# Moving the x buffers by 64 bytes in SBUF with two unused tiles

## The chip, the cores and the metric

The kernel runs on one core of a Trainium2 chip. The metric is device time in microseconds (us), the median over timed runs; less is better. One more execution is taken with the hardware profiler, and its trace is what is read below. The engines are named as in the profile: PE (TensorE, matmuls), PEld (TensorE's weight loads, which run beside its matmuls), DVE (VectorE), ACT (ScalarE), POOL (GpSimd), SP (SyncE, which issues most DMAs).

## What is computed

A gated linear attention over 768 positions (2 batches, 8 heads of 40), and behind it two feed-forward layers on 1536 tokens of width 320 with an inner width of 2048. All arrays are fp32.

```python
def reference(**kwargs):
    attn_out = _attn_ref(q, k, v, i_gate, f_gate, o_gate)        # a scan over t with gates
    x = attn_out.transpose(0, 2, 1, 3).reshape(1536, 320)
    h = x @ w_in                                                 # layer 1: 320 -> 2048
    g = np.where(h >= 1, h, np.where(h <= -1, 0.0, (h + 1) ** 2 / 4))
    x = g @ w_out                                                # 2048 -> 320
    h = x @ w2_in                                                # layer 2
    g = np.maximum(h, 0.0) + np.log1p(np.exp(-np.abs(h)))
    return g @ w2_out
```

## The kernel before, in words

**Split operands.** Each matmul of the feed-forward layers works on fp32 numbers that are split in a high and a low part, and sums three products: high by high, high by low, low by high. x has its high part in the tiles xh0 to xh2 and its low part in xl0 to xl2, one pair for each block of 512 tokens. A weight tile w holds the high parts of one of 16 slices of the inner width (384 columns for the way up, 320 for the way down) and behind them the low parts. The activations g are split into gh and gl (`split_g`, L811).

**The loops.** `steps` (L929) runs over the 2 layers, in each over the 3 blocks, in each over the 16 slices. A step has these parts:

- `up` (L756): 8 matmuls into one PSUM tile h, all recorded under L767. Each streams 512 columns of xh or xl against a 128 by 128 piece of w, which a weight load has put in place. TensorE loads the piece for the next matmul while the present one streams.
- the activation on ACT and DVE (`hinge` or `softplus`), and `split_g`.
- three steps later (`LAG`) the way down. In layer 1 `down1` (L826) has 8 matmuls (L836 to L842) that stream 512 columns of gh or gl against pieces of w, and sum in the PSUM tile D. In layer 2 `down2` (L880) has 12 (L897 to L899) that stream 320 columns of w against pieces of gh or gl, into A and D.

So the three kinds of matmuls differ in what streams: x in `up`, gh and gl in `down1`, w in `down2`.

**Handing over a block.** After the last `down1` of a block, `to_x` (L845) writes its sum back into xh and xl by ACT (L853, L861) and DVE (L857, L865), and only then may the next block's `down1` write D.

**The order.** All instructions stand in an order that the class `Plan` works out in advance with costs of its own (`plan.run`, L976); it knows nothing of addresses. Each engine then takes its list in that order and waits on semaphores.

**Where tiles lie.** A pool gets its place in SBUF when it is opened, and the tiles of a pool lie one behind another in the order of the code, so the x tiles lie in the pool `const` behind the tiles of L232 to L241, and raw, v, w, u, gh, gl in pools behind `const`. A row of xh or xl that one matmul streams is 512 x 4 = 2048 bytes in a partition, a piece of w or gh that one load fetches 128 x 4 = 512 bytes, and the parts of w begin at multiples of 256 bytes in it. An operand therefore begins at the same place modulo 256 as its tile.

The lines of `up` that name its operands, and the declaration of the x tiles:

```python
            ops = [(w[:, a + 128 * k:a + 128 * k + 128], xs) for k in range(2)
                   for a, xs in ((0, xh[j][:, k]), (0, xl[j][:, k]), (lo, xh[j][:, k]))]
            ops += [(w[:, a + 256:a + 384], xh[j][:, 2]) for a in (0, lo)]
            for i, (a, x) in enumerate(ops):
                nc.tensor.matmul(hp, a, x, start=(i == 0), stop=(i == len(ops) - 1))
...
    state = const.tile([128, H, V1], F32)
    xh = [const.tile([128, 3, n], F32R, name=f"xh{j}") for j, (_, n) in enumerate(BLOCKS)]
    xl = [const.tile([128, 2, n], F32R, name=f"xl{j}") for j, (_, n) in enumerate(BLOCKS)]
```

Of the kernel before, what the change touches and what calls it, by code (L numbers as in the profile page):

```python
# [7 lines left out]
F32 = mybir.dt.float32  # L8
# [201 lines left out]
def mlstm_moe_moe(ctx: ExitStack, tc: tile.TileContext, gates, late, qk, tok, ident, w1, w2, out):  # L210
    nc = tc.nc

    def pool(name, bufs, stack=ctx, **kw):
        return stack.enter_context(tc.tile_pool(name=name, bufs=bufs, **kw))
# [5 lines left out]
    const = pool("const", 1)  # L220
# [17 lines left out]
    gr = const.tile([128, EARLY * C], F32)  # L238
    is_col = const.tile([128, NC, H], F32)
    state = const.tile([128, H, V1], F32)  # L240
    xh = [const.tile([128, 3, n], F32R, name=f"xh{j}") for j, (_, n) in enumerate(BLOCKS)]  # L241
    xl = [const.tile([128, 2, n], F32R, name=f"xl{j}") for j, (_, n) in enumerate(BLOCKS)]
    scr_d = [dram.tile([n, 16, C], F32, name=f"scr_d{s}") for s, n in enumerate((4, 8))]
    scr_f = dram.tile([NC - EARLY, 16, C], F32)

# [816 lines left out]
```

## Time and profile before

| | us |
|---|---|
| median of 3 runs | 432.34 |
| lowest, highest | 432.06, 433.53 |
| span of the profiled execution | 429.5 |
| PE busy in it | 409.7 |
| DVE busy | 295.2 |
| ACT busy | 260.1 |

The median lies 2.8 us above the profiled span. The page of the profile gives busy times, and the chain of work that ended last: from the last instruction back, at each step to what released it. A busy matmul row is longer than what a matmul costs in a stream of them, because matmuls overlap in the pipeline; the cost of one is the distance from its start to the next one's start, and that is what is read below from the chain and from the timeline.

The execution has four stages: to about 60 us attention with the first matmuls of layer 1; from there to 113 us attention, layer 1 and the weights' DMAs together; from 113 to 263 us layer 1; from 263 to 424 us layer 2; then 5.5 us for the last output.

### The profile page before, as it was taken

What the parts mean: (1) busy time and instruction counts of PE and PEld (TensorE: products, weight loads), DVE (VectorE), ACT (ScalarE), POOL (GpSimd) and SP (SyncE); (2) the same over time, 40 slices, a digit from 0 to 9 for tenths busy, and PEclk for the clock granted to TensorE, in tenths of its full rate; (3) what the DMA queues carried; (4) which work ended last, traced back from release to release, by engine and by line L of the source; (5) the groups of instructions that cost most, each with busy time, mean ns of one, the idle gap of its engine ahead of it and who ended that gap; (6) DMA issues with size and microseconds to landing.
All of it is one profiled execution on the core that took longest, in us unless ns stands there. A gap on an engine that the chain in (4) does not pass through costs nothing.

```text
span 429.5 us, 8096 instructions
## 1 busy us (share of the span) xinstructions
PE 409.7 (95%) x3299; PEld 340.3 (79%) x3299; DVE 295.2 (69%) x479; ACT 260.1 (61%) x447; POOL 37.2 (9%) x46
## 2 busy tenths in 40 slices
PE   7988779999899999999999999999999999999994
PEld 5555558877788888887888888999989999899994
DVE  4687998999868556556878787655565555655552
ACT  3255867768666446889889755555555555555551
POOL 3333122213101000000000000000000000000001
PEclk9999969999999999999999999999999999999999
DMA  8979595797912001644344000000020000110002
GB/s 289 343 260 318 156 295 177 213 321 221 304 66 74 2 2 51 193 162 136 134 134 137 0 2 0 1 2 0 2 61 2 0 2 0 36 27 2 0 2 61
DMA packets 13685, 44.93 MB, mean 105 GB/s; under 512 B 2320, under 2 KB 3984, under 8 KB 13648
## 3 DMA queue, kind: packets, MB, share of 16 engines
q1 hardware_dynamic: 12832, 43.22, 31.2%
q10 hardware_dynamic: 752, 1.03, 0.9%
q8 instruction: 26, 0.43, 0.4%
q0 software_dynamic: 64, 0.16, 0.2%
q14 instruction: 11, 0.09, 0.1%
HBM read 42.36 MB, written 2.05 MB: 103 GB/s over the span
## 4 chain that ended last, share of the span: by engine, by line
PE 77%; DMA 8%; DVE 6%; ACT 4%; issue 1%; SPq 1%; POOL 0%; DVEq 0%; POOLq 0%
PE h L767 36%; DMA raw<-in_w_dram 5%; PE D L841 4%; PE D L840 4%; PE D L842 4%; PE D L897 3%; PE D L899 3%; PE D L898 3%; PE A L898 3%; PE A L899 3%; PE A L897 3%; PE D L836 2%; PE D L837 2%; DMA f<-scr_f 2%; ACT v L715 1%
## 5 line engine op out<-in xcount | busy, mean ns | idle before, releaser
L767 PE MATMUL h<-xh,w 128*128 128x512 f32 x576 | 182.6, 400 | 1.5 <-DVE w L747 1.1
L767 PEld LDWEIGHTS h<-xh,w 128*128 128x128 f32 x576 | 108.7, 189 | 26.8 <-DVE w L747 3.0
L820 DVE TENSOR_TENSOR gl<-u,gh 128x512 fp32r<-128x512 f32 x96 | 67.5, 704 | 39.6 <-ACT gh L816 38.4
L816 ACT CAST gh<-u 128x512 fp32r<-128x512 f32 x96 | 59.4, 619 | 46.7 <-DVE u L807 34.0
L767 PE MATMUL h<-xl,w 128*128 128x512 f32 x192 | 76.3, 397 | 1.4 <-DVE xl L698 1.4
L807 DVE TENSOR_TENSOR u<-u,e 128x512 f32<-128x512 f32 x48 | 33.3, 693 | 29.2 <-ACT e L803 29.2
L803 ACT ACTIVATE e<-e 128x512 f32<-128x512 f32 x48 | 30.3, 632 | 37.6 <-DVE e L798 37.6
L775 ACT ACTIVATE u<-h 128x512 f32<-128x512 f32 x48 | 28.5, 595 | 25.9 <-PE h L767 25.6
L767 PEld LDWEIGHTS h<-xl,w 128*128 128x128 f32 x192 | 36.4, 190 | 8.0 <-DVE xl L698 1.8
L784 DVE SCALAR_TENSOR_TENSOR u<-u,h 128x512 f32<-128x512 f32 x48 | 32.7, 682 | 13.9 <-ACT u L780 13.7
L841 PE MATMUL D<-gh,w 128*128 128x512 f32 x96 | 37.9, 395 | 0.0
L840 PE MATMUL D<-gh,w 128*128 128x512 f32 x96 | 37.8, 394 | 0.0
L842 PE MATMUL D<-gl,w 128*128 128x512 f32 x96 | 37.5, 391 | 0.0
L798 DVE SCALAR_TENSOR_TENSOR e<-u,h 128x512 f32<-128x512 f32 x48 | 33.0, 687 | 6.0 <-ACT u L794 1.0
L726 DVE SCALAR_TENSOR_TENSOR v<-raw,v 128x704 int32<-128x704 int32 x32 | 28.6, 895 | 9.8 <-ACT v L719 8.8
L794 ACT ACTIVATE u<-h 128x512 f32<-128x512 f32 x48 | 28.7, 598 | 10.6 <-PE h L767 10.3
L747 DVE TENSOR_TENSOR w<-v,w 128x64 fp32r<-128x64 f32 (+2 forms) x45 | 30.2, 701 | 2.4 <-ACT w L738 2.4
L715 ACT ACTIVATE v<-raw 128x704 f32<-128x704 int8 x32 | 27.1, 849 | 7.3 <-DMA raw<-in_w_dram 5.4
L780 ACT ACTIVATE u<-u 128x512 f32<-128x512 f32 x48 | 30.2, 630 | 0.4
L897 PE MATMUL D<-w,gh 128*128 128x320 f32 x96 | 29.6, 309 | 0.1
L899 PE MATMUL D<-w,gl 128*128 128x320 f32 x96 | 29.7, 309 | 0.0
L898 PE MATMUL A<-w,gh 128*128 128x320 f32 x96 | 29.7, 309 | 0.0
(120 smaller groups left out, 611.5 us busy)
## 6 DMA issues: line engine op xcount, KB each, us to landing
raw<-in_w_dram SPq DMA_DIRECT2D x32, 704.0 KB, 4.8
qx<-in_qk_dram SPq DMA_DIRECT2D x12, 640.0 KB, 7.2
tok<-in_tok_dram SPq DMA_DIRECT2D x12, 496.0 KB, 6.0
dec<-scr_d SPq DMA_DIRECT2D x16, 128.0 KB, 6.7
f<-scr_f SPq DMA_DIRECT2D x16, 128.0 KB, 6.7
out_dram<-o SPq DMA_DIRECT2D x20, 80.0 KB, 2.1
dec<-scr_d ACTq DMA_DIRECT2D x6, 128.0 KB, 7.0
consts<-in_ident_dram SPq DMA_DIRECT2D x1, 164.0 KB, 4.0
```

The source lines that it names most:

```text
L767: nc.tensor.matmul(hp, a, x, start=(i == 0), stop=(i == len(ops) - 1))
L784: nc.vector.scalar_tensor_tensor(out=tiles[U], in0=tiles[U], scalar=1.0, in1=tiles[HP], op0=ALU.min, op1=ALU.max)
L798: nc.vector.scalar_tensor_tensor(out=new("e", E, [128, n]), in0=tiles[M], scalar=-2.0, in1=tiles[HP], op0=ALU.mult, op1=ALU.add)
L807: nc.vector.tensor_tensor(out=tiles[M], in0=tiles[M], in1=tiles[E], op=ALU.add)
L816: nc.scalar.copy(new("gh", GH, [128, n], F32R), tiles[G])
L820: nc.vector.tensor_tensor(out=new("gl", GL, [128, n], F32R), in0=tiles[G], in1=tiles[GH].bitcast(F32), op=ALU.subtract)
L840: nc.tensor.matmul(d[i], hi[:, k], gh, start=s, stop=False)
L841: nc.tensor.matmul(d[i], lo[:, k], gh, start=False, stop=False)
L842: nc.tensor.matmul(d[i], hi[:, k], gl, start=False, stop=e)
L897: nc.tensor.matmul(d, gh[:, k], hi, start=s, stop=False)
L898: nc.tensor.matmul(d, gh[:, k], lo, start=False, stop=False)
L899: nc.tensor.matmul(d, gl[:, k], hi, start=False, stop=e)
```

## The change

```diff
     state = const.tile([128, H, V1], F32)
+    const.tile([128, 16], F32, name="gap0")
     xh = [const.tile([128, 3, n], F32R, name=f"xh{j}") for j, (_, n) in enumerate(BLOCKS)]
     xl = [const.tile([128, 2, n], F32R, name=f"xl{j}") for j, (_, n) in enumerate(BLOCKS)]
+    const.tile([128, 48], F32, name="gap1")
```

Two tiles are declared in `const` that nothing reads or writes: 64 bytes in a partition ahead of the x tiles, 192 bytes behind them. In the built programs the tiles begin at these bytes of a partition:

| tile | before | modulo 256 | after | modulo 256 |
|---|---|---|---|---|
| xh0 | 23360 | 64 | 23424 | 128 |
| xl0 | 41792 | 64 | 41856 | 128 |
| raw, first | 54080 | 64 | 54336 | 64 |
| w, slice 0 of layer 1 | 121728 | 128 | 121984 | 128 |
| gh, first | 167296 | 128 | 167552 | 128 |
| gl, first | 175488 | 128 | 175744 | 128 |

All xh and xl tiles share the place of xh0 modulo 256, and all tiles of w, gh and gl that of the first. So the x tiles move by 64 bytes; all that lies behind them moves by 256 and keeps its place modulo 256; all ahead of them stays. No instruction is added, taken away or moved: the lists of all five engines, with their waits, are the same in both programs but for line numbers (up by one or two) and the numbers in names.

## Rows read from the trace of the kernel before

**Rows 1.** The page: busy time by engine, and shares of the chain that ended last.
```profile
PE 409.7 (95%) x3299; PEld 340.3 (79%) x3299; DVE 295.2 (69%) x479; ACT 260.1 (61%) x447; POOL 37.2 (9%) x46
...
PE 77%; DMA 8%; DVE 6%; ACT 4%; issue 1%; SPq 1%; POOL 0%; DVEq 0%; POOLq 0%
```

**Rows 2.** Windows, three stages: length, busy (instructions) by engine, PEclk, DMA share, GB/s.
```profile
183.30:200.22 16.92, 16.64 (x72) 13.16 (x72) 10.15 (x15) 14.38 (x25) 0.00 (x0) 1.00 0.54 174
200.22:262.88 62.66, 62.52 (x278) 51.08 (x278) 50.02 (x73) 48.76 (x80) 1.71 (x1) 1.00 0.20 70
262.88:424.04 161.16, 161.12 (x899) 145.72 (x899) 94.39 (x139) 82.89 (x137) 0.58 (x1) 1.00 0.04 9
```

**Rows 3.** Windows of line 767 alone (`up`): busy and count of matmuls, of loads.
```profile
60.00:113.06 53.06, 20.98 (x78) 14.04 (x76) 0.97 0.78 241
113.06:183.30 70.24, 36.03 (x142) 26.43 (x142) 1.00 0.27 86
183.30:200.22 16.92, 9.98 (x40) 7.49 (x40) 1.00 0.54 174
200.22:262.88 62.66, 32.29 (x128) 23.98 (x128) 1.00 0.20 70
262.88:424.04 161.16, 86.81 (x344) 62.98 (x344) 1.00 0.04 9
```

**Rows 4.** Windows of line 836 alone (once in each `down1`).
```profile
113.06:183.30 70.24, 6.91 (x17) 3.20 (x17) 1.00 0.27 86
...
200.22:262.88 62.66, 6.31 (x16) 2.97 (x16) 1.00 0.20 70
```

**Rows 5.** The chain in time, layer 1: start us, length us, what.
```profile
204.14 1.86 PE h L767 x8
...
252.24 1.86 PE h L767 x8
...
255.94 3.73 PE h L767 x16
```

**Rows 6.** The chain in time, layer 2.
```profile
263.58 1.86 PE h L767 x8
...
328.55 1.85 PE h L767 x8
...
415.12 1.86 PE h L767 x8
```

**Rows 7.** Timeline of PE, a `down1` behind another: start us, modelled length, what.
```profile
85.03 0.39 PE L840 MATMUL D<-gh,w 128*128 128x512 f32 x1
85.27 0.39 PE L841 MATMUL D<-gh,w 128*128 128x512 f32 x1
...
85.72 0.39 PE L836 MATMUL D<-gh,w 128*128 128x512 f32 x1
...
87.53 0.39 PE L767 MATMUL h<-xh,w 128*128 128x512 f32 x1
```

**Rows 8.** Timeline of PE: `down1`, `up`, `down1`, and the first of the next `up`.
```profile
202.16 0.39 PE L836 MATMUL D<-gh,w 128*128 128x512 f32 x1
...
203.97 0.39 PE L767 MATMUL h<-xh,w 128*128 128x512 f32 x1
...
205.84 0.39 PE L836 MATMUL D<-gh,w 128*128 128x512 f32 x1
...
207.67 0.39 PE L767 MATMUL h<-xh,w 128*128 128x512 f32 x1
```

**Rows 9.** The chain in time, where layer 1 hands a block over.
```profile
183.31 0.60 ACT u L775
...
187.62 5.42 DMA raw<-in_w_dram
...
200.22 0.47 PE D L836
```

**Rows 10.** Groups of ACT by line and form: writes into gh and into xh.
```profile
L816 ACT CAST gh<-u 128x512 fp32r<-128x512 f32 x96 | 59.4, 619 | 46.7 <-DVE u L807 34.0 <-DVE u L784 12.4
...
L861 ACT CAST xh<-D 128x512 fp32r<-128x512 f32 x6 | 3.5, 585 | 1.7 <-DVE xl L865 1.5 <-PE D L842 0.2
```

## The prediction

> **What bounds the kernel now.** I read the page first: PE is busy for 95% of the span and makes 77% of the chain that ended last [rows 1]. Next the windows by stage: from 200 us to 424 us PE is busy in 223.64 of 223.82 us, with its clock granted in full and DVE and ACT at 80% of the time or less [rows 2]. There only a shorter matmul stream shortens the kernel. So the question is what one matmul costs in the stream, start to start, and the chain and the timeline show that.
>
> In layer 1 a step of eight `up` and eight `down1` matmuls takes (252.24 - 204.14) / 13 = 3.700 us, of which `up` takes 3.73 / 2 = 1.865 [rows 5], leaving 1.835 for `down1`. [...] In layer 2 a step takes (415.12 - 263.58) / 42 = 3.608 us, with about 1.855 for the eight `up` (the rows alternate between 1.85 and 1.86) [rows 6] and 1.753 for the twelve `down2`, which is 146.1 ns each.
>
> **Which matmuls are slow.** The three kinds give the test that the change needs, since before it they already differ in the place of the streamed rows modulo 256: x at 64, but gh, gl and w at 128, with all loaded pieces at 128. The timeline around 204 us has both in a row: eight streams of gh and gl take 203.97 - 202.16 = 1.81 us, the following eight of x 205.84 - 203.97 = 1.87, the next eight of gh and gl 207.67 - 205.84 = 1.83 [rows 8]. A `down1` that follows another `down1`, with no x around it, takes 87.53 - 85.72 = 1.81 us [rows 7], 226 ns a matmul against 233 for x. [...] The 1.83 of a `down1` right behind an `up` reads like a return to the settled state.
>
> **The change part by part.**
>
> The tiles themselves add no instruction, and the order and the waits of all engines are unchanged. Cost 0.
>
> The writes into x land at 128 instead of 64. Two casts of one shape bound that: 585 ns into xh at 64, 619 ns into gh at 128 [rows 10]. They read from different memories, so the 34 ns is an upper bound; below, nothing excludes the same size as a gain. Six such writes stand in the hand-overs, two or three on the chain in each, so 0.1 us either way. I take 0.
>
> The `up` streams are the main term. I take the settled `down1` as their new cost, 1.81 us for eight [rows 7], because after the change stream and load stand exactly as there. On the path I count the stretches where the chain is PE's: 113.06 to 183.30 and 200.22 to 262.88 us with 142 + 128 = 270 matmuls, and layer 2 with 344 [rows 3].
> - Layer 1: 270 / 8 = 33.75 groups x (1.865 - 1.81 = 0.055) = 1.86 us.
> - Layer 2: 43 groups x (1.855 - 1.81 = 0.045) = 1.94 us.
>
> The `down1` behind them should also stay settled, since nothing ahead of it disturbs it: 17 + 16 = 33 groups [rows 4] x (1.835 - 1.81 = 0.025) = 0.83 us.
>
> The `down2` keep their places. Should they drop into the rhythm of `up`'s new neighbours I bound them by 0.5 ns each way, 12 x 43 x 0.5 ns = 0.26 us; I take 0.15 us as a loss.
>
> What doesn't count: before 113 us PE waits for weights, DMAs and attention, so 78 `up` matmuls from 60 us on [rows 3] give nothing, 9.75 x 0.055 = 0.54 us at the most. And from 183.31 to 200.22 us the chain runs over ACT, one DMA of 5.42 us and DVE to the first `down1` of the next block [rows 9]; PE's 40 `up` and some five `down1` there only make it wait longer, so their 5 x 0.055 + 5 x 0.025 = 0.4 us is not gained. The same hand-over into layer 2, at 262.88, is covered by 16 `up` matmuls; they shrink by 0.11 us and PE waits that much longer. I take 0.1 us off.
>
> **Sum.** 1.86 + 1.94 + 0.83 - 0.15 - 0.1 = 4.4 us off the profiled span: 429.5 - 4.4 = 425.1. The median of the runs lies 2.8 us above that span, so the forecast is 432.34 - 4.4 = 427.9, told as 428.0 us. With what I left out (0.54 + 0.4) it would be 427.0.
>
> [...]
>
> **The rivals.**
>
> *Half.* `up` loads pieces at the start and at the low half of w in turn, and `down1` also has single slow steps although its places agree, 0.24 us from 85.03 to 85.27 [rows 7]. If the average of an `up` becomes that of a `down1` in the steps of layer 1, 1.835, and `down1` stays: 33.75 x 0.03 + 43 x 0.02 = 1.9 us, so 430.5 us. For it speaks that 1.835 is the mean over thirteen steps; against it, that `down1` reaches 1.81 when it follows its own kind.
>
> *No effect.* The extra cycles of x come from something else that sets x apart: its distance from w, far ahead in SBUF, or its eight sums into one PSUM tile. Then the change doesn't do what it says, and the time is 432.3. [...]
>
> [...]
>
> **How the numbers follow.** The forecast (428.0) has 0.60, half 0.13, no effect 0.15, slower 0.12. The range runs from 426.8, the sum with all that I left out and 0.2 us of spread between runs, to 432.4, which takes in half and no effect; about 0.12 lies above, and some 0.05 below or between. A measurement here can tell about 0.3%, which is 1.3 us, from no change. The forecast falls below 431.0 nearly always, half two times in three; so faster 0.68, same 0.20 (no effect, a third of half, and a little of both ends), slower 0.12.
>
> **What would show it.** In the trace after, the eight `up` matmuls of a step should take 1.81 us start to start in both layers, `down1` 1.81, `down2` 1.75 for twelve; the step of layer 1 should fall from 3.700 to 3.62 and that of layer 2 from 3.608 to 3.56. The wait ahead of the first `down1` near 200 us should be longer by up to 0.4 us. The forecast is wrong if `up` stays at 1.86 (no effect), goes to 1.83 (half) or above 1.87 (slower), or if it falls as said and the span doesn't, in which case a wait for ACT or DVE has taken PE's place between 200 and 263 us, where they are busiest.

## The result and the profile after

The median after is 428.23 us over 22 runs, against 432.69 us for the kernel before over as many runs beside it: a ratio of 0.991, with a 95% interval from 0.9885 to 0.9935. The profiled execution has a span of 425.2 us, against 429.5. A second timing, below, gave 0.993 (0.9893 to 0.9967). The medians are over all runs; a ratio leaves out the runs that fell in a slower state, 2 of the 22 of the changed kernel.

In the chain of layer 1 after the change (start us, length us, what), the eight `up` matmuls take 1.81 us and a step (248.71 - 201.56) / 13 = 3.627 us; the rows of before are [rows 5], with 1.86 and 3.700. Lines are numbered two higher than before.

```profile
201.56 1.81 PE h L769 x8
...
248.71 1.81 PE h L769 x8
252.34 3.63 PE h L769 x16
...
259.17 0.41 PE D L899
```

The timeline of PE has one `up` and one `down1` behind it; each matmul follows the one before at 0.22 to 0.23 us, with no difference between the two kinds. The same place before is [rows 8].

```profile
205.03 0.39 PE L769 MATMUL h<-xh,w 128*128 128x512 f32 x1
205.25 0.39 PE L769 MATMUL h<-xl,w 128*128 128x512 f32 x1
...
206.84 0.39 PE L838 MATMUL D<-gh,w 128*128 128x512 f32 x1
207.07 0.39 PE L839 MATMUL D<-gl,w 128*128 128x512 f32 x1
...
208.65 0.39 PE L769 MATMUL h<-xh,w 128*128 128x512 f32 x1
```

Layer 2 is the exception. In its chain the eight take 1.84 us, where before they took 1.86 or 1.85 [rows 6], and a step takes (410.78 - 263.45) / 41 = 3.593 us instead of 3.608.

```profile
263.45 1.84 PE h L769 x8
...
410.78 1.84 PE h L769 x8
...
419.69 0.50 DVE o L913
```

The timeline of one such step shows where it is lost: the first two streams take 0.23 and 0.24 us, and only the last ones 0.227 ((333.41 - 332.73) / 3), as in layer 1 (1.81 / 8 = 0.226).

```profile
331.57 0.39 PE L769 MATMUL h<-xh,w 128*128 128x512 f32 x1
331.80 0.40 PE L769 MATMUL h<-xl,w 128*128 128x512 f32 x1
332.04 0.62 PE L769 MATMUL h<-xh,w 128*128 128x512 f32 x2
332.50 0.39 PE L769 MATMUL h<-xl,w 128*128 128x512 f32 x1
332.73 0.84 PE L769 MATMUL h<-xh,w 128*128 128x512 f32 x3
333.41 0.30 PE L899 MATMUL D<-w,gh 128*128 128x320 f32 x1
```

### The profile page after: what moved, and what is told of

Read it like the earlier page. It is cut to its first block, busy times and chain, and to the rows that moved or that the text cites. A ratio compares the mean times of both kernels' runs of the same rounds, so it can differ in the third digit from the quotient of the medians.

```text
span 425.2 us, 8096 instructions
## 1 busy us (share of the span) xinstructions
PE 405.1 (95%) x3299; PEld 339.5 (80%) x3299; DVE 294.9 (69%) x479; ACT 259.9 (61%) x447; POOL 38.7 (9%) x46
## 4 chain that ended last, share of the span: by engine, by line
PE 83%; DVE 5%; DMA 5%; ACT 3%; SPq 2%; issue 1%; POOL 0%; DVEq 0%; POOLq 0%
PE h L769 37%; PE D L844 4%; PE D L842 4%; PE D L843 4%; PE D L899 3%; PE D L901 3%; PE D L900 3%; PE A L901 3%; PE A L900 3%; PE A L899 3%; PE D L838 2%; PE D L839 2%; DMA raw<-in_w_dram 2%; DMA f<-scr_f 2%; PE fill L462 1%
## 5 line engine op out<-in xcount | busy, mean ns | idle before, releaser
L769 PE MATMUL h<-xh,w 128*128 128x512 f32 x576 | 179.6, 395 | 1.3 <-DVE w L749 0.8
L842 PE MATMUL D<-gh,w 128*128 128x512 f32 x96 | 37.4, 390 | 0.0
L843 PE MATMUL D<-gh,w 128*128 128x512 f32 x96 | 37.4, 390 | 0.0
L901 PE MATMUL A<-w,gl 128*128 128x320 f32 x96 | 29.7, 309 | 0.0
```

What stands on the lines that cost most here:

```text
L842: nc.tensor.matmul(d[i], hi[:, k], gh, start=s, stop=False)
L843: nc.tensor.matmul(d[i], lo[:, k], gh, start=False, stop=False)
L901: nc.tensor.matmul(d, gl[:, k], hi, start=False, stop=e)
```

## The experiments

All shift tiles by unused bytes and leave every instruction and wait as it is. Below, "difference" is the place of a stream less that of the loads beside it, modulo 256. Three theories were open: the difference counts; the stream's own place counts; the load's own place counts.

**All operands at 64.** Against the kernel before, only the tile behind xl is added:

```diff
     xl = [const.tile([128, 2, n], F32R, name=f"xl{j}") for j, (_, n) in enumerate(BLOCKS)]
+    const.tile([128, 48], F32, name="gap1")
```

> The x tiles stay at 64 modulo 256 as in the kernel before; the 192 unused bytes behind them bring w, gh and gl down to 64 as well, so that all operands lie at 64. If the difference between the places of stream and load counts (theory): as the changed kernel, eight up matmuls of layer 1 in 1.81 us, eight down1 in 1.81, a step of layer 1 in 3.63 us and of layer 2 in 3.59, time near 428 us. If the stream's own place counts (rival, a stream that begins at 64 is slow): up stays at 1.865, down1 rises to 1.865, down2 to about 1.84 for twelve, and the time rises to about 435 us.

The chain of this kernel, layer 1 and layer 2:

```profile
203.32 1.81 PE h L768 x8
...
217.83 1.81 PE h L768 x8
...
265.24 1.84 PE h L768 x8
...
412.59 1.84 PE h L768 x8
```

Ratio 0.9923 (0.9879 to 0.9968), median 428.77 us. x lies where it lay before the change, and the gain is there all the same, with the same exception in layer 2. So it isn't x's own place that cost, and no distance in SBUF either; the difference counts.

**gh and gl 64 bytes further on, in both layers.** (So is xr behind them, which no matmul reads.)

```diff
     for name in ("raw", "v", "w", "u", "gh", "gl", "xr"):
+        if name == "gh":
+            pool("gap_gh", 1).tile([128, 16], F32, name="gap_gh")
         pools[name] = pool(name, BUFS[name])
```

> The changed kernel with 64 unused bytes more between u and gh, so that gh and gl lie at 192 modulo 256 while x and w stay at 128. If the difference counts: up that is not next to a way down stays near 1.81 us for eight, down1 (streams gh at 192, loads w at 128) rises to about 1.865, down2 (streams w at 128, loads gh at 192) loses some 16 cycles more in each, 153 ns instead of 146, so a step of layer 2 gets 0.08 us longer; time about 433 us. If the stream's own place counts: down1 1.865, down2 stays at 146 ns. If the load's own place counts: down1 stays at 1.81, down2 rises to 153 ns.

The 7 ns by which a `down2` was to rise are those between 233 ns for a matmul of `up` (3.73 / 16) [rows 5] and 226 for a settled one of `down1` (1.81 / 8) [rows 7]. A cycle is taken here as the time of one column, an estimate: the 226 ns of 512 columns less the 146 of 320, over 192 columns, 0.42 ns; 16 of them are 7 ns.

Timeline of PE, one `down1` of layer 1 between two `up`:

```profile
217.98 0.39 PE L771 MATMUL h<-xh,w 128*128 128x512 f32 x1
...
219.80 0.40 PE L840 MATMUL D<-gh,w 128*128 128x512 f32 x1
...
221.65 0.39 PE L771 MATMUL h<-xh,w 128*128 128x512 f32 x1
```

`down1` rose to 221.65 - 219.80 = 1.85 us. The load's own place would have left it at 1.81; the difference raises it, if not quite to the 1.865 expected (x at the same +64 costs 3.68 / 2 = 1.84 us for eight, below). The second half of the expectation failed: a step of layer 2 takes 3.587 us by its rows below ((413.09 - 266.02) / 41), less than the 3.593 of the changed kernel, and not 0.08 more. Twelve `down2` take 146 ns each although their loads lie 64 bytes above the streams. Taken alone, this run fits the stream's own place best (`down1` up, `down2` as it was); that theory fails in the run before, with all operands at 64, and so the difference is shown for the streams of 512 columns only. The time, 429.25 us (ratio 0.9903, interval 0.9861 to 0.9946), decides nothing here.

```profile
266.02 1.83 PE h L771 x8
...
413.09 1.83 PE h L771 x8
```

**x at other places.** Four kernels move x alone; only the sizes of the two gaps differ.

```diff
-    const.tile([128, 16], F32, name="gap0")
+    const.tile([128, 48], F32, name="gap0")      # x at 0; 32 for x at 192, 8 for 96, 24 for 160
...
-    const.tile([128, 48], F32, name="gap1")
+    const.tile([128, 16], F32, name="gap1")      # and 32, 56, 40
```

> Unused tiles of 192 and 64 bytes, so x lies at 0 modulo 256, the rest stays at 128: the difference is 128 bytes. If only agreement is cheap: up near 1.865 us for eight or above, down1 as before (1.835 a step), time 432 us. If the places count modulo 128: up 1.81 as in the changed kernel, time 428 us.

> Unused tiles of 128 bytes each, so x lies at 192 modulo 256, 64 bytes above the loads instead of 64 below. If only agreement is cheap: up near 1.865 us for eight, time 432 us. If the sign of the difference counts (the loads run ahead of or behind the stream): another value, between 1.81 and 1.90.

> Unused tiles of 32 and 224 bytes, so x lies at 96 modulo 256, 32 bytes below the loads. [...] If places within one 64-byte stretch count as agreeing or not by where they begin: 1.81 or 1.865.

> Unused tiles of 96 and 160 bytes, so x lies at 160 modulo 256, 32 bytes above the loads. [...] If places within one 64-byte stretch count as one: 1.81, as in the changed kernel.

One row of the chain of each, sixteen `up` matmuls with no way down between them. First x at 0 (difference 128):

```profile
255.60 3.73 PE h L769 x16
```

x at 192 (64 above the loads):

```profile
253.50 3.68 PE h L769 x16
```

x at 96 (32 below):

```profile
256.92 3.73 PE h L769 x16
```

x at 160 (32 above):

```profile
254.67 3.74 PE h L769 x16
```

These stand beside 3.73 for 64 below [rows 5] and 3.63 for no difference, all in profiled executions with a mean granted clock of 0.991 to 0.996. A matmul costs 233 or 234 ns at 128, -64, -32 and +32, 230 at +64, and 227 at 0. The cost does not grow with the difference, and half of 64 bytes is no better than the whole. Of the places tried, agreement alone is cheap; that +64 lies between the two is the second case that its expectation allowed, that the sign counts. All that lies behind x has moved by 256 bytes here too, so that move is not what helps. The 3.73 at 128 also shows that agreement modulo 128 is not enough; modulo 256 is, for in the changed kernel gh and w agree modulo 512 as well (167552 - 121984 = 89 x 512) while x and w do not (121984 - 23424 = 385 x 256; in layer 1 all pieces of w begin at multiples of 512 bytes in it), and both kinds take 1.81 us for eight. These are single profiles, and the four times, 428.6 to 432.8 us, are single runs that say nothing beyond the rows.

**Layer 2: left over from `down2`, or `up`'s own?** The row of sixteen in the changed kernel's chain, 3.63 us at 252.34, is already layer 2's: 424 of the 768 `up` matmuls start ahead of the first `down2`, and 384 are layer 1's. So they run with layer 2's weights, at the settled cost. That points to `down2`. The test moves gh in layer 2 alone, which no `up` touches.

```diff
-            nc.scalar.copy(new("gh", GH, [128, n], F32R), tiles[G])
+            new("gh", GH, [128, n + 64], F32R)
+            tiles[GH] = tiles[GH][:, 16 * l:16 * l + n]      # 48 * l, 32 * l in the others
+            nc.scalar.copy(tiles[GH], tiles[G])
```

> The changed kernel, in which layer 2 alone keeps gh 64 bytes further on (192 modulo 256; gl, x and w at 128). The up matmuls of layer 2 keep their own places. If the slow first steps of up in layer 2 are left over from the down2 ahead of it: their pattern 231, 236, 228, 232, 231, 227 ns changes, and eight up take another time than 1.84 us, by the run with gh and gl at 192 about 1.83. If up's own operands in layer 2 make it: 1.84 us and the pattern stay. Layer 1 stays at 3.63 us a step, the time near 428 us either way.

```profile
263.26 1.81 PE h L769 x8
...
409.55 1.81 PE h L769 x8
```

> As the run before with gh of layer 2 at 64 modulo 256 (192 bytes further on), so the loads of gh lie 64 bytes below the streams of w. If the way down sets the first steps of up: again another pattern, somewhere from 1.81 to 1.87 us for eight, and by the run with x at 192 the streams of w lose up to 10 cycles more against two of three loads, 149 ns instead of 146. If not: 1.84 us and 146 ns.

```profile
265.84 1.84 PE h L769 x8
...
412.66 1.84 PE h L769 x8
```

> As the run with gh of layer 2 at 192, with gh at 0 modulo 256. If only the settled state that down2 leaves behind counts, some places leave it and some do not: eight up matmuls of layer 2 in 1.81 or 1.84 us, the step between 3.56 and 3.61 us. If the place 64 bytes on is the only good one: 1.84 us or more.

```profile
265.57 1.85 PE h L769 x8
...
412.90 1.85 PE h L769 x8
```

With gh at 192 the eight take 1.81 us, with gh at 64 1.84, at 0 1.85, and nothing of `up` was moved. The expectation of the first was too careful: 1.81 (but for two of the 43 rows, 1.84) and not 1.83. A step takes (409.55 - 263.26) / 41 = 3.568 us. The second came out the other way for `down2`: (412.66 - 265.84) / 41 - 1.84 = 1.741 us for twelve, 145 ns each and not 149. The third is the second case of its expectation: of the four places tried for gh, only 192 gives 1.81. With gh at 0 a step takes (412.90 - 265.57) / 41 = 3.593 us, as in the changed kernel, since `down2` takes less by what `up` takes more.

ACT writes gh and DVE reads it while PE works, so they could be what slows `up`. In the changed kernel they work on it at another time. The slow streams of the step shown above run from 331.57 to 332.73 us, and both engines' work on gh comes before and after that:

```profile
329.22 0.62 ACT L818 CAST gh<-u 128x512 fp32r<-128x512 f32 x1 [0.76 <-DVE u L809]
329.88 0.69 DVE L822 TENSOR_TENSOR gl<-u,gh 128x512 fp32r<-128x512 f32 x1 [0.69 <-ACT gh L818]
332.81 0.62 ACT L818 CAST gh<-u 128x512 fp32r<-128x512 f32 x1 [0.76 <-DVE u L809]
333.47 0.69 DVE L822 TENSOR_TENSOR gl<-u,gh 128x512 fp32r<-128x512 f32 x1 [0.69 <-ACT gh L818]
```

So where the gh lies that `down2` loads sets what the eight `up` behind it cost, 1.81, 1.84 or 1.85 us; this is argued by exclusion, and how it does so is not shown.

**Both kernels once more, and the better one timed.**

> The kernel before, profiled once more. If the 1.3 us that the changed kernel gained ahead of 113 us came by chance, the sixth-last up group of the first block starts somewhere within 2 us around 111.3 us, as in the other runs; if the change gives it, at 113.06 us again for the piece of six up matmuls in the chain. The stretch from the first down1 of the third block (200.22) to the first down2 step that waits (262.88) should again take 62.7 us, and layer 2 161.2.

> The changed kernel once more, timed and profiled. The streams give 3.0 us in the trace (2.4 from 113 to 263 us, 0.6 in layer 2), what comes ahead of 113 us is chance: ratio to the kernel before 0.993. If the early gain belongs to the change, 4.4 us: ratio 0.990.

> The changed kernel with gh of layer 2 at 192 modulo 256, timed. A step of layer 2 takes 3.568 us instead of 3.594, 43 of them 1.1 us: if that is all, 0.0026 below the ratio of the changed kernel, near 0.990 to the kernel before. If the wait for the last copies or the outputs takes it back: the ratio of the changed kernel.

Chain of the kernel before, profiled again:

```profile
121.00 3.73 PE h L767 x16
...
202.84 0.47 PE D L836
...
265.49 0.42 PE D L897
...
426.66 0.50 DVE o L911
```

Chain of the changed kernel, profiled again:

```profile
118.83 3.64 PE h L769 x16
...
199.52 0.47 PE D L838
...
261.02 0.42 PE D L899
...
421.58 0.50 DVE o L913
```

The same rows stood at 118.40, 200.22 [rows 9], 262.88 and 424.04 us in the first profile of before, and at 117.04, 197.69, 259.17 and 419.69 in the first of after. So, for the stretch from the row of sixteen to the last copy:

| stretch | before | before again | after | after again |
|---|---|---|---|---|
| up to the row of sixteen | 118.40 | 121.00 | 117.04 | 118.83 |
| to the third block's `down1` | 81.82 | 81.84 | 80.65 | 80.69 |
| to layer 2's D | 62.66 | 62.65 | 61.48 | 61.50 |
| to the last copy | 161.16 | 161.17 | 160.52 | 160.56 |

What comes behind 118 us repeats within 0.1 us, and the change takes 2.9 to 3.0 us off it. What comes ahead of it differs by 2.6 us between two profiles of one program and by 1.8 between two of the other. The 1.36 us by which the first pair differed there are inside that spread. The other kernels say the same: the row of sixteen starts at 116.61 to 121.00 us in the six profiles in which x and w disagree, and at 116.64 to 119.45 us in seven in which they agree.

The sign that the expectation of the kernel before had named did not come: the piece of `up` that stood at 113.06 us in the first profile starts at 114.16 us, later than either case. A part of that has a cause that the trace shows. PE issues nothing for 2.80 us from 108.73 us on, and soon after, from 113.0 to 116.4 us, its clock was granted at 0.52 on average. The eight `up` that begin there take 3.17 us instead of 1.87. Two rows of its chain:

```profile
108.73 2.80 issue
...
114.16 3.17 PE h L767 x8
```

And the row of that window, in the columns of [rows 2]:

```profile
113.00:116.40 3.40, 3.40 (x49) 2.83 (x42) 3.37 (x8) 1.57 (x2) 0.82 (x1) 0.52 0.63 203
```

The kernel with gh of layer 2 at 192 was timed at 428.12 us, a ratio of 0.9915 (0.9876 to 0.9954), beside 429.61 and 0.993 for the changed kernel in the same runs. The intervals overlap, so the time alone doesn't part the two. The trace does: from the third block's `down1` to the last copy it takes 420.98 - 199.96 = 221.02 us by its chain, the changed kernel 222.00 and 222.06, the kernel before 223.82 twice. The 1.0 us is near the 1.1 expected.

```profile
199.96 0.47 PE D L840
...
420.98 0.50 DVE o L915
```

## Why the prediction was right, and where it was not

The time came out as forecast, 428.2 against 428.0 us, and the span as well, 425.2 against 425.1. The cause was right, but the largest term was about three times too large, smaller ones missed both ways, and chance made up for it.

- **What bounds the kernel, and the reading of the three kinds of streams: right.** Shorter streams shortened the kernel, and no engine took PE's place: from 197.69 to 419.69 us after the change PE is busy in 221.84 of 222.00 us, by the rows below (columns as in [rows 2]). That agreement of places was the cause, and not something else about x, is shown by the run with all operands at 64. It also ends the rivals *no effect* (432.3 us) and *slower* (`up` above 1.87 us). Why the places count is not shown; the same stream of x, at the same bytes, costs 1.865 us for eight with its loads at 128 [rows 5] and 1.81 with them at 64.

```profile
197.69:259.17 61.48, 61.35 (x278) 51.12 (x278) 49.93 (x73) 48.64 (x80) 1.71 (x1) 1.00 0.21 71
259.17:419.69 160.52, 160.49 (x899) 145.66 (x899) 94.31 (x139) 82.80 (x137) 0.58 (x1) 1.00 0.04 9
```

- **`up` in layer 1: right.** 1.81 us for eight was forecast and measured. The row of sixteen in [rows 5] that gave 1.865 belongs to layer 2's first slices; the eight of layer 1 cost the same.
- **`down1`: right.** The step fell from 3.700 to 3.627 us where 3.62 was forecast, so `down1` takes 3.627 - 1.81 = 1.82 and has lost its unsettled start.
- **`up` in layer 2: wrong.** The step that failed is the sentence that takes the settled `down1` as the new cost "because after the change stream and load stand exactly as there". They do, but what a stream costs also depends on the matmuls ahead of it, and in layer 2 these are a `down2`. The term was 1.94 us, less 0.15 for `down2`, and no run shows the 0.5 ns a matmul behind that: `down2` takes (3.593 - 1.84) / 12 = 146.1 ns, as before. The stretch gave 161.16 - 160.52 = 0.64, 3.608 - 3.593 = 0.015 us a step. The prediction had seen such a leftover in `down1` behind `up`, 1.83 us for 1.81 [rows 8], and didn't ask whether `up` behind `down2` has one. The 1.84 us for eight come near the 1.835 of the rival *half*, but by luck: its reason would have shown in the steps of layer 1, where `up` took 1.81 and `down1` became shorter too.
- **The hand-over into the third block: half right.** The wait at its `down1` grew from 0.28 to 0.40 us, as forecast, but the 0.4 us from 183 to 200 us were not all lost. In the chain after, PE leads to 193.68 us and ACT and DVE only from there, so most of what PE saved up to there counts. Ahead of it the sum was too high. It had 17.75 x 0.055 + 17 x 0.025 = 1.40 us from 113 to 183 us and nothing from there to 200. Measured from the row of sixteen at 118 us, it is (177.71 - 118.40) - (175.53 - 117.04) = 0.82 us up to the piece of `up` at 177.71 us, by the rows below, and 1.17 up to this `down1`: about half a microsecond less than counted ahead of 183 us, and a part of that given back by the hand-over.

```profile
175.53 1.81 PE h L769 x8
...
193.70 0.59 ACT xh L863
...
197.69 0.47 PE L838 MATMUL D<-gh,w 128*128 128x512 f32 x1 [0.40 <-DVE xl L867]
```

And before:

```profile
177.71 1.86 PE h L767 x8
...
200.22 0.47 PE L836 MATMUL D<-gh,w 128*128 128x512 f32 x1 [0.28 <-DVE xl L865]
```

- **From there to layer 2: the number right, two terms not.** 16 groups x (0.055 + 0.025) - 0.1 = 1.18 us were counted, and 62.66 - 61.48 = 1.18 measured. But a step gained 3.700 - 3.627 = 0.073 us and not 0.08, and the 0.1 us were not lost: from the row of sixteen to D it is 262.88 - 255.94 = 6.94 us before and 259.17 - 252.34 = 6.83 after. The sixteen `up` are on the chain there, and PE does not wait longer by what they save. The two misses cancel.
- **Ahead of 113 us: right to count nothing.** The profile showed 1.3 us less there, which is inside the spread of the repeats and of the other kernels. Without it the span would have been some 426.5 us. The streams alone give 3.0 us of 432.3, a ratio of 0.993. That lies inside both intervals of the changed kernel, but so does the 0.990 that 4.4 us would give: the times don't decide between the two, the chains do, and by them the sum of 4.4 was about half too much. The range allowed 0.2 us of spread between runs, while the three runs of before already lay 432.06 to 433.53 us; that the median came out within 0.3 us of the forecast is luck.

## What to carry to other kernels

Where TensorE runs back to back and each matmul loads new fp32 weights, as here, compare start to start, not busy time, for matmuls of one shape that differ only in where their operands lie; two kinds side by side in one trace are a test that needs no run. For streams of 512 columns, try streamed tiles and weight tiles at the same place modulo 256 (here 1.81 us for eight, and 1.865 with 64 bytes between) and look at the trace again, since the kind of matmul ahead also counts (1.84 behind `down2` in the changed kernel); the streams of 320 columns here gained nothing from it (146 ns each either way). Take a cost that was read in one neighbourhood to another only after looking for a leftover from the neighbour.

## What was not expected of the hardware

- A stream of 512 columns with a load beside it costs 227 ns when their places agree (3.63 us for sixteen), and up to 234 when they don't; 32 bytes off cost as much as 64 below or 128 (3.74, 3.73 and 3.73 us), and 64 above less (3.68).
- The streams of 320 columns in `down2` do not follow that: 146 ns at agreement, 146 with loads 64 bytes above, 145 with two of three loads 64 bytes below. Whether it is their length that matters is open.
- Where gh lies in layer 2 changes the cost of the `up` that follows, which doesn't touch gh: 1.81, 1.84 and 1.85 us for eight with gh at 192, 64 and 0. In the changed kernel neither ACT's writes nor DVE's reads of gh run beside the slow streams (331.57 to 332.73 us in the step shown). How the place of gh acts on `up` the rows don't show.
